# Decode attention with a streamed K and V cache: 64 KB rows in overlapping places instead of 32 KB rows in a ring of four

## The chip, the cores and the metric

The kernel runs on one core of one Trainium2 chip. The metric is the device time of one execution in microseconds. Before the change the median of three runs is 2530.58 us (2530.54 to 2530.72).

## What is computed

One token passes through two branches that a gate mixes: attention over a cache of 65536 keys and values for each of 32 heads, and a small gated MLP. The cut reference:

```python
def _A_ref(x, k_cache, v_cache, wq, wo):      # H = 32, Dh = 128, Sk = 65536, D = 512
    q = (x @ wq).reshape(B, Sq, H, Dh).transpose(0, 2, 1, 3)
    scores = jnp.einsum("bhqd,bhkd->bhqk", q, k_cache) * (Dh ** -0.5)
    p = _softmax(scores, axis=-1)
    o = jnp.einsum("bhqk,bhkd->bhqd", p, v_cache)
    return o.transpose(0, 2, 1, 3).reshape(B, Sq, H * Dh) @ wo

def _B_ref(x, w_gate, w_up, w_down):          # F = 1792
    return (_silu(x @ w_gate) * (x @ w_up)) @ w_down

g = _sigmoid((x * gate_w).sum(-1, keepdims=True))
return g * a + (1 - g) * b
```

All tensors are bf16. K and V hold 512 MiB each; every byte of them is read once, for one query row.

## The kernel before

**The stream.** K and V of a head are cut into four tiles (`t` = 0 to 3) of 4 MB. In a tile each of the 128 partitions holds `ROWS` = 128 successive keys of 128 numbers, one contiguous row of 32 KB in HBM. `ring` has `NPL` = 4 places of 32 KB in each partition. `plan_stream` (L26) writes the order of all loads by hand: wq, the first K tile, the MLP's weights, the other K tiles of head 0, then for each head h from 1 on its K tiles alternating with the V tiles of head h - 1, and at the end the four V tiles of the last head. Load n goes to place n mod 4. The loop L63 to L86 notes for each place the tile that it held before; the last three V tiles are cut in parts by `ENDS`, so that little is left to do after the last one lands.

**The issuing queue.** All loads are issued by SP, in order (`issue`, L190). Ahead of each it waits until the tile that held the place is worked off: a K tile by `ktdone` (its two transposes are done), a V tile by `pvdone` (its matmuls are done), a weight by the semaphore of its last use. Two tiles of K and two of V are in the ring at a time. The sixteen DMA engines work on one queue; an engine carries eight of a DMA's 128 rows and then a packet of 4 bytes that raises the semaphore.

**K.** DVE (`head_k`, L365) waits for a K tile and transposes it in two units of `UROWS` = 64 rows into `kt`, which has two buffers; a unit waits until PE has finished with the unit two before it (`qkdone`). PE (`scores`, L435) takes 16 matmuls for each unit, all 128 of a head accumulating in `psS`.

**Softmax.** After a head's last unit DVE takes the maximum over `psS` (`head_max`), GpSimd the maximum over partitions, ACT the exponential (`head_exp`), GpSimd the sum. `head_turn` transposes the probabilities on DVE after the first unit of the next head's K; `head_norm` takes the reciprocal of the sum after the fourth.

**V.** PE (`values`, L456) takes 32 matmuls of four rows each for a V tile, accumulating a head in `psO`. ACT scales the result (`row_norm`), PE turns it into a column (`turn`, L478), ACT stores the column. PE's loop (L519) runs `scores(1, t)` and `values(0, t)` in turn, so head h's V is worked off between the tiles of head h + 1's K.

**Start and end.** At the start PE computes q from wq; the MLP sits between units of head 0 (`mlp_up` after the first, `mlp_down` after the second). At the end the output weights wo are loaded into `kt` after the first V tile of the last head (L205), and `regroup`, `project_groups` and `project` multiply the heads' columns by them. The last V tile's matmuls go directly to the column `psT` (L473).

Of the kernel before, what the change touches and what calls it, by code (L numbers as in the profile page):

```python
# [5 lines left out]
P = 128  # L6
ROWS = 128
UROWS = 64
PLACE = ROWS * 128
UNIT = UROWS * 128  # L10
NPL = 4
NSEM = 8
STEP = 16
ENDS = {1: (64, 128), 2: (64, 128), 3: (64, 96, 112, 128)}
# [9 lines left out]


def plan_stream(H, PL):  # L26
    first = [("wq",), ("k", 0, 0), ("wg", "wu"), ("wd",)]
    first += [("k", 0, t) for t in range(1, PL)]
    steady = [(kind, h - d, t) for h in range(1, H) for t in range(PL) for kind, d in (("k", 0), ("v", 1))]
    last = [("v", H - 1, t) for t in range(PL)]  # L30
    return first, steady, last


def bass_gated_mix__mha_block_cached__swiglu_ffn__decode_kernel(
# [18 lines left out]
    PL = S // P // ROWS  # L53
    UN = 2 * PL
# [3 lines left out]
    assert Dh == 128 and D == 512 and F % P == 0 and PL == 4  # L58

    first, steady, last = plan_stream(H, PL)  # L60
    items = first + steady + last

    dmas = []  # L63
    landed = {}
    place = {}
    owner = [None] * NPL
    for n, item in enumerate(items):
        s = n % NPL
        if item[0] in "kv":
            place[item] = s  # L70
            parts = [(0, ROWS)]
            if item[:2] == ("v", H - 1) and item[2] in ENDS:
                parts = list(zip((0,) + ENDS[item[2]], ENDS[item[2]]))
            for r0, r1 in parts:
                landed[item + (r1,)] = len(dmas)
                dmas.append((item, r0, r1, s, owner[s]))
        else:
            for j, name in enumerate(item):
                place[name] = (s, j)
                landed[name] = len(dmas)  # L80
                dmas.append(((name,), 0, 0, s, owner[s]))
        owner[s] = item
        if item == ("v", H - 1, 0):
            for name in ("woa", "wob"):
                landed[name] = len(dmas)
                dmas.append(((name,), 0, 0, None, None))  # L86

    with ExitStack() as ctx:
# [6 lines left out]
        def sem(name):  # L95
# [9 lines left out]
        ring = sb("ring", [P, NPL, PLACE], BF16)  # L105
# [28 lines left out]

        tail = landed[("v", H - 1, 0, ROWS)]
        ds = [sem(f"ds{i}") for i in range(NSEM + len(dmas) - tail)]
        (s_x, s_ones, s_sel0, s_sel, s_unit0, s_unit, s_z, s_e1, s_xT, s_xTb, s_q, s_qTb, s_qs, s_qd, s_qz,
         s_qw, s_h, s_sig, s_gu, s_b, s_dch, ktdone, qkdone, pvdone, s_mx, s_ar, s_nb, expdone, s_pb, s_L,
         s_li, s_or, s_zr, s_zb, s_z4, s_sel4, s_x1, s_x2, s_pt, s_oc, s_otn, s_y, s_fin, s_out) = [sem(n) for n in (
             "s_x s_ones s_sel0 s_sel s_unit0 s_unit s_z s_e1 s_xT s_xTb s_q s_qTb s_qs s_qd s_qz "  # L140
             "s_qw s_h s_sig s_gu s_b s_dch ktdone qkdone pvdone s_mx s_ar s_nb expdone s_pb s_L "
# [16 lines left out]
        def weight(name):  # L158
            s, j = place[name]
            n = w_dram[name].shape[1]  # L160
            return ring[:, s, j * n:(j + 1) * n]

        wq_ap = weight("wq").rearrange("p (c n) -> p c n", c=Dc)
        wg_ap = weight("wg").rearrange("p (c m j) -> p c m j", c=Dc, j=FC)
        wu_ap = weight("wu").rearrange("p (c m j) -> p c m j", c=Dc, j=FC)
        wd_ap = weight("wd").rearrange("p (c n) -> p c n", c=FC)
        ktf = kt[:].rearrange("p b t -> p (b t)").bitcast(BF16)
        woa = ktf[:, 0:HN * D].rearrange("p (b m) -> p b m", b=HB)
        wob = ktf[:, HN * D:].rearrange("p (h n) -> p h n", n=D)
        ktb = [kt[:, b, :].bitcast(BF16).rearrange("p (j k m e) -> p j k m e", j=2, k=4, e=2) for b in range(2)]  # L170
# [3 lines left out]
        def counts(n):  # L174
            return (ds[n % NSEM], 16 * (n // NSEM + 1)) if n < tail else (ds[NSEM + n - tail], 16)

        def arrived(eng, n, more=0):
            sem_n, count = counts(n)
            eng.wait_ge(sem_n, count + more)  # L179

        def pv(h, t):
            return STEP * (h + 1) + 4 * (t + 1)
# [3 lines left out]
        @block.sync  # L186
        def _(sp):
            k_dram, v_dram = [c.rearrange("a h (b p r) d -> (a h b) p (r d)", p=P, r=ROWS) for c in (A_k_cache, A_v_cache)]

            def issue(n, q0=0):  # L190
                item, r0, r1, s, old = dmas[n]
                name = item[0]
                if old is not None and r0 == 0:
                    if old[0] == "k":
                        sp.wait_ge(ktdone, STEP * old[1] + 4 * (old[2] + 1) + 4 * q0)
                    elif old[0] == "v":
                        sp.wait_ge(pvdone, pv(old[1], old[2]) + 4 * q0)
                    else:
                        sp.wait_ge({"wq": s_q, "wg": s_h, "wd": s_b}[old[0]], 1)
                if name in ("k", "v"):  # L200
                    cache = k_dram if name == "k" else v_dram
                    src = cache[bass.ds(PL * item[1] + item[2] + q0, 1), :, r0 * Dh:r1 * Dh].rearrange("q p m -> (q p) m")
                    dst = ring[:, s, r0 * Dh:r1 * Dh]
                elif name in ("woa", "wob"):
                    sp.wait_ge(qkdone, STEP * H)  # L205
                    dst, src = (woa if name == "woa" else wob), wo_dram[name]
                else:
                    dst, src = weight(name), w_dram[name]
                sp.dma_start(dst, src).then_inc(counts(n)[0], 16)  # L209
                if n == 0:  # L210
                    sp.dma_start(xrow[0:1, :], xr_dram).then_inc(s_x, 16)  # L211
                    sp.dma_start(gwrow[0:1, :], gw_dram).then_inc(s_x, 16)  # L212

            turn_round = landed[("k", 2, 0, ROWS)]
            for n in range(turn_round):
                issue(n)
            with sp.Fori(0, PL * (H - 3) + 1, PL) as q0:
                for n in range(turn_round, turn_round + 2 * PL):
                    issue(n, q0)
            for n in range(tail, len(dmas)):  # L220
                issue(n)
# [29 lines left out]
        def _(act):  # L251
# [10 lines left out]
            def row_norm(h, more=0):  # L262
                act.wait_ge(s_li, STEP * (h + 1) + more)
                act.wait_ge(pvdone, pv(h, PL - 1) + more)
                act.wait_ge(s_pt, STEP * (h + 1) + more)
                nc.scalar.mul(orow[0:4, :], psO[0:4, :], Li[0:4, :]).then_inc(s_or, STEP)  # L266
# [32 lines left out]
            act.wait_ge(pvdone, pv(H - 1, PL - 2))  # L299
# [8 lines left out]
        def _(dve):  # L308
# [46 lines left out]
            def head_turn(h, more=0):  # L355
                dve.wait_ge(expdone, STEP * (h + 1) + more)
                dve.wait_ge(pvdone, pv(h - 1, PL - 1) + more)
                nc.vector.transpose(pb[:], pa[:]).then_inc(s_pb, STEP)  # L358
# [6 lines left out]
            def head_k(h, more=0):  # L365
                for u in range(UN):
                    i = h * UN + u
                    if u % 2 == 0:
                        arrived(dve, landed[("k", h, u // 2, ROWS)], more)
                    if i >= 2:  # L370
                        dve.wait_ge(qkdone, 2 * (i - 1) + more)  # L371
                    o = kt[:, i % 2, :].rearrange("p (j r t) -> p r j t", j=2, t=32)
                    src = ring[:, place[("k", h, u // 2)], (u % 2) * UNIT:(u % 2 + 1) * UNIT]
                    src = src.bitcast(U32).rearrange("p (r j t) -> p r j t", j=2, t=32)
                    nc.vector.transpose(o, src).then_inc(ktdone, 2)  # L375
                    if i == 1:
                        mlp_steps()
                    if u == 0 and h >= 1:
                        head_turn(h - 1, more)
                    if u == 3 and h >= 1:  # L380
                        head_norm(h - 1, more)
# [8 lines left out]
            dve.wait_ge(pvdone, pv(H - 1, PL - 1))  # L390
# [4 lines left out]
        def _(pe):  # L395
# [7 lines left out]
            arrived(pe, landed["wq"])  # L403
# [13 lines left out]
            def mlp_up():  # L417
                arrived(pe, landed["wg"])
                arrived(pe, landed["wu"])
# [7 lines left out]
            def mlp_down():  # L427
                arrived(pe, landed["wd"])
# [4 lines left out]
                done.then_inc(s_b, 1)  # L433

            def scores(h, t, more=0):  # L435
                for u in (2 * t, 2 * t + 1):
                    i = h * UN + u
                    pe.wait_ge(ktdone, 2 * (i + 1) + more)
                    if u == 0:
# [3 lines left out]
                    for k in range(4):  # L443
                        at0 = 31 - (4 * u + k)
                        for je in range(4):
                            done = nc.tensor.matmul(psS[:], qw[:, je, at0:at0 + 128],  # L446
                                                    ktb[i % 2][:, je // 2, k, :, je % 2],
                                                    start=(u == 0 and k == 0 and je == 0),
                                                    stop=(u == UN - 1 and k == 3 and je == 3))
                    done.then_inc(qkdone, 2)  # L450
                    if h == 0 and u == 0:
                        mlp_up()
                    if h == 0 and u == 1:
                        mlp_down()

            def values(h, t, more=0):  # L456
# [60 lines left out]
            for t in range(PL):  # L517
                scores(0, t)
# [47 lines left out]
```

## Time and profile before

| what | value |
|---|---|
| median of three runs | 2530.58 us |
| the profiled execution's own time | 2531.01 us |
| its span, first to last instruction | 2529.2 us |
| read from HBM | 1087.64 MB |
| PE busy, mean granted clock | 2028.8 us (80%), 0.927 |
| DVE busy | 1170.8 us (46%) |
| ACT busy, GpSimd busy | 69.0 us, 27.4 us |
| transposes of K (L375) | 256, 4424 ns each |
| matmuls of scores (L446) | 1080.7 us busy |
| matmuls of values (L468) | 898.6 us busy |
| maximum, exponential, probabilities' transpose | 32 each, 691, 687 and 671 ns |

Durations of single matmuls overlap, so the busy time of a group of them divided by their number says more than a matmul's own duration. The share of the DMA engines is a mean over all sixteen. The profiled execution's time stands beside its own span; the median is that of other executions.

### The profile page before, as it was taken

To read this page: it belongs to the slowest core of one execution; us is meant where nothing else is said; L and a number is where in the kernel's file an instruction comes from. 1 tells how busy PE (TensorE), PEld (TensorE's weight loads), DVE (VectorE), ACT (ScalarE), POOL (GpSimd) and SP (SyncE) were. 2 spreads that over 40 slices of the span, in tenths; PEclk is the share of its full clock that TensorE was granted. 3 is DMA by queue.
4 is the path that set the end of the run, shared out by engine and by line. 5 is a ranking of instruction groups with operands and counts; after the bars stand their busy time and mean duration, and the time that the engine had idled before them with its cause. 6 is when DMAs were issued, how large, how long until landed. Compare 5 with 4: busy or idle time off the path is not lost.

```text
span 2529.2 us, 20878 instructions
## 1 busy us (share of the span) xinstructions
PE 2028.8 (80%) x8736; PEld 813.5 (32%) x8864; DVE 1170.8 (46%) x374; ACT 69.0 (3%) x198; POOL 27.4 (1%) x80
## 2 busy tenths in 40 slices
PE   5888788787877877888778878787887788877888
PEld 3333233333333333333323333333333333333333
DVE  4644544454445444544454445444544454455441
ACT  0000000000000000000000000000000000000000
POOL 0000000000000000000000000000000000000000
PEclk9999989989999999899998998999999989999999
DMA  9999999999999999999999999999999999999999
GB/s 416 431 431 432 432 432 431 432 432 432 432 431 431 433 432 431 431 431 432 432 432 432 432 433 431 431 431 431 434 431 431 431 432 431 433 433 432 432 431 381
DMA packets 39614, 1087.78 MB, mean 430 GB/s; under 512 B 4275, under 2 KB 4790, under 8 KB 5942
## 3 DMA queue, kind: packets, MB, share of 16 engines
q1 hardware_dynamic: 39604, 1087.65, 100.0%
q8 instruction: 7, 0.11, 0.0%
q14 instruction: 1, 0.01, 0.0%
q10 hardware_dynamic: 2, 0.00, 0.0%
HBM read 1087.64 MB, written 0.00 MB: 430 GB/s over the span
## 4 chain that ended last, share of the span: by engine, by line
DMA 76%; DVE 12%; issue 11%; SPq 1%; PE 0%; DVEq 0%; ACT 0%
DMA ring<-in_A_k_cache_dram 75%; DVE kt L375 12%; DMA ring<-in_A_v_cache_dram 1%; SPq L209 1%; PE psS L446 0%; DVEq L371 0%; DVEq L362 0%; PE psY L491 0%; PE psT L473 0%; ACT fin L302 0%; SPq L211 0%; DVE oTn L391 0%; SPq L212 0%; DVEq L390 0%; DVEq L179 0%
## 5 line engine op out<-in xcount | busy, mean ns | idle before, releaser
L375 DVE STREAM_TRANSPOSE kt<-ring 128x4096 uint32<-128x4096 uint32 x256 | 1125.1, 4424 | 1142.5 <-DMA ring<-in_A_k_cache_dram 1138.7
L446 PE MATMUL psS<-kt,qw 128*128 128x512 bf16 x3968 | 1080.7, 431 | 478.2 <-DVE kt L375 472.9
L468 PE MATMUL psO<-ring,pb 128*4 128x512 bf16 x4064 | 898.6, 379 | 2.7 <-DMA ring<-in_A_v_cache_dram 2.7
L446 PEld LDWEIGHTS psS<-kt,qw 128*128 128x128 bf16 x4096 | 419.3, 106 | 1137.8 <-DVE kt L375 387.5
L468 PEld LDWEIGHTS psO<-ring,pb 128*4 128x4 bf16 x4064 | 343.4, 87 | 536.3 <-issue 41.2
L353 DVE TENSOR_REDUCE mxs<-psS 128x1 f32<-128x512 f32 x32 | 22.1, 691 | 142.6 <-PE psS L446 142.6
L260 ACT COPY qw<-qd 128x16 bf16 (+1 forms) x33 | 8.6, 260 | 2210.0 <-PE psS L446 2203.2
L246 POOL PARTITION_ALL_REDUCE amx<-mxs x32 | 11.3, 352 | 2397.4 <-DVE mxs L353 2397.4
L482 PEld LDWEIGHTS psT<-unit,orow 4*128 4x128 f32 x264 | 31.8, 186 | 15.2 <-issue 13.7
L482 PE MATMUL psT<-unit,orow 4*128 4x1 f32 x264 | 34.6, 248 | 0.9 <-ACT orow L300 0.5
L266 ACT ACTIVATE orow<-psO,Li 4x512 f32<-4x512 f32 x31 | 21.0, 679 | 138.4 <-PE psO L468 138.4
L358 DVE STREAM_TRANSPOSE pb<-pa 128x512 bf16<-128x512 bf16 x32 | 21.5, 671 | 6.3 <-PE psO L468 6.3
L280 ACT ACTIVATE pa<-psS,nbias 128x512 bf16<-128x512 f32 x32 | 22.0, 687 | 5.2 <-ACT nbias L276 5.1
L391 DVE TENSOR_SCALAR oTn<-psT,Li,zb 128x1 bf16<-128x1 f32 x1 | 0.3, 279 | 38.3 <-PE psT L473 38.3
L248 POOL PARTITION_ALL_REDUCE Lt<-rsum x32 | 12.3, 384 | 44.9 <-ACT pa L280 44.9
L400 PE MATMUL psM<-ones,xrow 1*128 1x1 bf16 x4 | 0.3, 172 | 13.3 <-DMA gwrow<-in_gate_w_dram 13.3
L270 ACT ACTIVATE oTn<-psT,zb 128x1 f32 (+1 forms) x32 | 8.2, 255 | 1.1 <-PE psT L482 1.1
L276 ACT ACTIVATE nbias<-amx 128x1 f32<-128x1 f32 x32 | 6.5, 203 | 33.3 <-POOL amx L246 33.3
L423 PEld LDWEIGHTS psM<-xTb,ring 128*128 128x128 bf16 x112 | 6.9, 161 | 0.2
L423 PE MATMUL psM<-xTb,ring 128*128 128x1 bf16 x112 | 6.8, 198 | 0.0
L510 PE MATMUL psY<-kt,oX 128*1 128x512 bf16 x28 | 6.2, 379 | 0.0
L280 ACT ACTIVATION_READ_ACCUMULATOR pa<-psS,nbias 128x1 f32 x32 | 6.2, 193 | 0.0
(51 smaller groups left out, 42.5 us busy)
## 6 DMA issues: line engine op xcount, KB each, us to landing
ring<-in_A_k_cache_dram SPq DMA_DIRECT2D x128, 4096.0 KB, 29.7
ring<-in_A_v_cache_dram SPq DMA_DIRECT2D x125, 4096.0 KB, 27.7
ring<-in_A_v_cache_dram SPq DMA_DIRECT2D x5, 2048.0 KB, 23.5
ring<-in_A_wq_dram SPq DMA_DIRECT2D x1, 4096.0 KB, 12.3
kt<-in_A_wo_dram SPq DMA_DIRECT2D x1, 3584.0 KB, 14.7
ring<-in_B_w_gate_dram SPq DMA_DIRECT2D x1, 1792.0 KB, 26.0
ring<-in_B_w_up_dram SPq DMA_DIRECT2D x1, 1792.0 KB, 29.8
ring<-in_B_w_down_dram SPq DMA_DIRECT2D x1, 1792.0 KB, 33.6
```

The costliest lines, as they stand in the source:

```text
L209: sp.dma_start(dst, src).then_inc(counts(n)[0], 16)
L246: nc.gpsimd.partition_all_reduce(amx[:], mxs[:], P, RMAX).then_inc(s_ar, STEP)
L248: nc.gpsimd.partition_all_reduce(Lt[:], rsum[:], P, RADD).then_inc(s_L, STEP)
L266: nc.scalar.mul(orow[0:4, :], psO[0:4, :], Li[0:4, :]).then_inc(s_or, STEP)
L280: nc.scalar.activation(pa[:], psS[:], ACT.Exp, bias=nbias[:], scale=SCALE, accum_out=rsum[:]).then_inc(expdone, STEP)
L353: nc.vector.reduce_max(mxs[:], psS[:], AX_X).then_inc(s_mx, STEP)
L358: nc.vector.transpose(pb[:], pa[:]).then_inc(s_pb, STEP)
L375: nc.vector.transpose(o, src).then_inc(ktdone, 2)
L423: done = nc.tensor.matmul(psM[:, o + j:o + j + 1], w[:, c, :, j], xTb[:, c:c + 1], start=(c == 0), stop=(c == Dc - 1))
L446: done = nc.tensor.matmul(psS[:], qw[:, je, at0:at0 + 128], ktb[i % 2][:, je // 2, k, :, je % 2], start=(u == 0 and k == 0 and je == 0), s ...
L468: done = nc.tensor.matmul(psO[0:4, :], pbk[:, k, rho:rho + 4], v[:, r * Dh:(r + 4) * Dh], start=(t == 0 and r == 0), stop=(t == (PL - 1 if ...
L482: done = nc.tensor.matmul(psT[:, 0:1], orow[0:4, i * Dh:(i + 1) * Dh], unit[0:4, i:i + 1], start=(i == 0), stop=(i == 3 and h < H - 1))
```

## The change

K and V no longer share a ring. K has `kr`, 96 KB in each partition, V has `vr`, 80 KB. A head's K and V come in two tiles (`b` = 0, 1) of 8 MB, a row of 64 KB (256 keys) in each partition. The two places of K lie at 0 and at 32 KB of `kr` and share 32 KB; the two places of V lie at 0 and at 16 KB of `vr` and share 48 KB. So a tile can be loaded when the shared part of the tile before it is worked off, and the tiles are worked off with this part first: `K_ORDER` for K, in eight units of 32 rows (`UP` = 8), and `V_ORDER` for V, in quarters of 64 rows. `kt` shrinks by half with the unit, and `ktdone`, `qkdone` and `pvdone` count finer steps; `pv(h, n)` stands for n of head h's eight quarters of V. SP's order is written out: in the loop K b=0, V b=0, K b=1, V b=1, one wait ahead of each.

Head 0's K comes in four halves of 4 MB, the first two ahead of the MLP's weights, which go to `vr`, and the third one behind a wait for four units. The MLP's matmuls all come after the twelfth unit of head 0. The output weights go to `kr`, ahead of the last head's V, which comes in parts (`LAST`); its first tile goes to K's second place. `turn` now follows a head's first unit, and the end runs regroup, the projections and then the last head's values.

The diff, cut to its core:

```diff
+HALF = 128
+ROWS = 2 * HALF
+UROWS = 32
+QROWS = 64
+K_AT = (0, PLACE // 2)
+V_AT = (0, PLACE // 4)
+V_ORDER = ((1, 2, 3, 0), (0, 1, 2, 3))
+LAST = {0: (128, 192, 256), 1: (64, 128, 192, 224, 240, 256)}
...
+    K_ORDER = (tuple(range(UP // 2, UP)) + tuple(range(UP // 2)), tuple(range(UP)))
...
-        ring = sb("ring", [P, NPL, PLACE], BF16)
+        kr = sb("kr", [P, 3 * PLACE // 2], BF16)
+        vr = sb("vr", [P, 5 * PLACE // 4], BF16)
...
-            turn_round = landed[("k", 2, 0, ROWS)]
-            for n in range(turn_round):
-                issue(n)
-            with sp.Fori(0, PL * (H - 3) + 1, PL) as q0:
-                for n in range(turn_round, turn_round + 2 * PL):
-                    issue(n, q0)
-            for n in range(tail, len(dmas)):
-                issue(n)
+            load(("wq",), w_at["wq"], w_dram["wq"])
+            sp.dma_start(xrow[0:1, :], xr_dram).then_inc(s_x, 16)
+            sp.dma_start(gwrow[0:1, :], gw_dram).then_inc(s_x, 16)
+            first_k(0, HALF, ROWS)
+            first_k(0, 0, HALF)
+            load(("wg",), w_at["wg"], w_dram["wg"])
+            sp.wait_ge(ktdone, UP // 2)
+            first_k(1, 0, HALF)
+            load(("wu",), w_at["wu"], w_dram["wu"])
+            load(("wd",), w_at["wd"], w_dram["wd"])
+            first_k(1, HALF, ROWS)
+            with sp.Fori(0, 2 * (H - 2) + 1, 2) as q0:
+                more = q0 * (STEP // 2)
+                for b in range(2):
+                    sp.wait_ge(ktdone, STEP + (-UP // 2, UP // 2)[b] + more)
+                    load(("k", b), k_rows(b, 0, ROWS), cache_rows(k_dram, 1, b, 0, ROWS, q0))
+                    sp.wait_ge(pvdone, (pv(-1, 7), pv(0, 3))[b] + more)
+                    load(("v", b), v_rows(0, b, 0, ROWS), cache_rows(v_dram, 0, b, 0, ROWS, q0))
+            sp.wait_ge(ktdone, STEP * (H - 1) + UP)
+            load(("woa",), woa, wo_dram["woa"])
+            load(("wob",), wob, wo_dram["wob"])
+            sp.wait_ge(ktdone, STEP * H)
+            for b in range(2):
+                if b == 1:
+                    sp.wait_ge(pvdone, pv(H - 2, 8))
+                for r0, r1 in zip((0,) + LAST[b], LAST[b]):
+                    load(("vl", b, r1), v_rows(H - 1, b, r0, r1), cache_rows(v_dram, H - 1, b, r0, r1))
...
             def head_k(h, more=0):
-                for u in range(UN):
-                    i = h * UN + u
-                    if u % 2 == 0:
-                        arrived(dve, landed[("k", h, u // 2, ROWS)], more)
+                for n in range(UN):
+                    i = h * UN + n
+                    b, w = n // UP, K_ORDER[n // UP][n % UP]
+                    if h == 0 and n % (UP // 2) == 0:
+                        dve.wait_ge(landing(("k0", b, w * UROWS)), 16)
+                    if h > 0 and n % UP == 0:
+                        dve.wait_ge(landing(("k", b)), 16 * h + more)
                     if i >= 2:
-                        dve.wait_ge(qkdone, 2 * (i - 1) + more)
+                        dve.wait_ge(qkdone, i - 1 + more)
...
-                for r in range(0, ROWS, 4):
...
+                order = V_ORDER[b] if h < H - 1 else (0, 1, 2, 3)
+                if h < H - 1:
+                    pe.wait_ge(landing(("v", b)), 16 * (h + 1) + more)
+                for n, c in enumerate(order):
+                    for r in range(c * QROWS, (c + 1) * QROWS, 4):
...
+                    done.then_inc(pvdone, 2)
...
             with pe.Fori(0, STEP * (H - 1), STEP) as more:
-                for t in range(PL):
-                    scores(1, t, more)
-                    if t == 0:
-                        turn(-1, more)
-                    values(0, t, more)
+                for b in range(2):
+                    scores(1, b, more)
+                    values(0, b, more)
```

## The prediction

> **What bounds the kernel now.** I read the page's slices first, then the queue's share, the chain of waits, and last the waits of the issuing queue. In the slices and the queue table one resource has no free tenth:
>
> ```profile
> span 2529.2 us, 20878 instructions
> PE   5888788787877877888778878787887788877888
> DVE  4644544454445444544454445444544454455441
> DMA  9999999999999999999999999999999999999999
> DMA packets 39614, 1087.78 MB, mean 430 GB/s; under 512 B 4275, under 2 KB 4790, under 8 KB 5942
> q1 hardware_dynamic: 39604, 1087.65, 100.0%
> DMA 76%; DVE 12%; issue 11%; SPq 1%; PE 0%; DVEq 0%; ACT 0%
> ```
>
> PE and DVE have holes in every slice; the sixteen DMA engines have none. The chain lies on K landings. Its DVE and issue shares are no cost of their own: during them the issuing queue SP is ahead of the engines. The waits of SP from 400 to 2400 us, and the issue table, show by how much:
>
> ```profile
> SPq L209 <- PE psO L468: 1153.5, 103, 13.0
> SPq L209 <- DVE kt L375: 730.7, 103, 8.6
> ring<-in_A_k_cache_dram SPq DMA_DIRECT2D x128, 4096.0 KB, 29.7
> ring<-in_A_v_cache_dram SPq DMA_DIRECT2D x125, 4096.0 KB, 27.7
> ```
>
> A 4 MB DMA lands 28 to 30 us after its issue, and the stream gives one about every 9.7 us, so about two others are ahead of each: the queue never runs dry. So only two things can move the time: the time an engine needs per byte, and a hole in the queue. The stream's pace is read where DVE starts a head, on a K landing:
>
> ```profile
> 1008.88 4.45 DVE L375 STREAM_TRANSPOSE kt<-ring 128x4096 uint32<-128x4096 uint32 x1 [5.51 <-DMA ring<-in_A_k_cache_dram]
> 1086.60 4.45 DVE L375 STREAM_TRANSPOSE kt<-ring 128x4096 uint32<-128x4096 uint32 x1 [5.14 <-DMA ring<-in_A_k_cache_dram]
> 1164.34 4.45 DVE L375 STREAM_TRANSPOSE kt<-ring 128x4096 uint32<-128x4096 uint32 x1 [5.14 <-DMA ring<-in_A_k_cache_dram]
> 1242.06 4.45 DVE L375 STREAM_TRANSPOSE kt<-ring 128x4096 uint32<-128x4096 uint32 x1 [6.02 <-DMA ring<-in_A_k_cache_dram]
> ```
>
> (1242.06 - 1008.88) / 3 = 77.73 us a head, eight DMAs of 4 MB, 9.716 us each: 431.7 GB/s. On one engine such a DMA is eight packets of 32 KB and one of 4 bytes that raises the semaphore.
>
> **What a packet costs beyond its bytes.** I read the trace's packet records, start to start on one engine: 1214 ns for 32 KB and 611 ns for 16 KB (the last V places); 308.6 ns for 8 KB and 156.4 ns for 4 KB. The 4-byte packet pushes the next one back by 6 ns: 8 x 1214 + 6 = 9718, the 9.716 us above. Two packets of 16 KB take 2 x 611 - 1214 = 8 ns more than one of 32 KB. Averaged over all records of the two sizes the difference is 6.8 ns, and two 8 KB against one of 16 KB give 6.7. The records' own durations (1217.5 and 615 ns) would give 12.5, but they overlap the next start by 3 to 4 ns. So a packet costs 7 to 12.5 ns whatever its size; I take 8, since the starts are what the stream goes by.
>
> The Trainium skill, "DMA: Bandwidth & Descriptors", section "Why small descriptors are slow (HBM only)", has a fixed cost of about 3 cycles a packet besides 32 bytes of descriptor. At that page's 850 MHz and 27.2 bytes per ns I estimate 4.7 ns, which would make the gain 5.4 us where mine is 8.7; the starts in this trace are dearer than the page.
>
> **The change, part by part.**
>
> *Rows of 64 KB in the loop.* 31 rounds of four DMAs are 124 DMAs of 8 MB, in place of 248 of 4 MB. The trace of before has no 64 KB packet. Bounds for what each engine saves per 8 MB: below, nothing but the second semaphore packet, 6 ns; above, 8 x 12.5 + 6 = 106 ns. Taken: 8 x 8 + 6 = 70 ns, since 64 KB continues the row of sizes. Times 124: 8.7 us, with ends 0.7 and 13.1. Head 0, the weights and the last V keep 32 KB rows or smaller, in the same sizes and number as before.
>
> *Places free by parts.* One DMA is in flight and one is queued, where about two were. An 8 MB DMA takes 19.36 us. The costs at nothing hold only while SP gets each next DMA out early, so I work out both waits from a K landing at 0. From issue to first packet take 1.3 us (SP's first issue at 0.73, its packets from 1.76 on), and from the last packet to the landing seen by an engine up to 1.5 us (packets behind the first K start at 21.6 to 22.6, DVE at 24.07).
>
> K's second place waits for four units of 32 rows on DVE: half of the 4424 ns of the transpose group each, 8.8 us. It must be issued by 19.4 - 1.5 - 1.3 = 16.6: 7.8 us to spare. The V place loaded after it waits for three quarters of the V before: PE starts these when the eight units of scores are done, at 8 x 2.2 + 1.9 (eight matmuls, 3.78 us for sixteen) + 1.05 for turn = 20.6, then 48 matmuls at 221 ns (898.6 us / 4064): 31.2. It must be issued by 38.7 - 2.8 = 35.9: 4.7 to spare. The wait on V's second place has the same sum without turn. Queued behind either wait on SP is only the next DMA, whose own wait ends later anyway. So zero, covered by the transfer in flight. At the head's end, reduce, all-reduce and exp take under 4 us (1080.77 to 1083.2) and their transpose of the probabilities comes after the first unit of the next K, 38 us on: covered.
>
> *DVE and PE in half units.* 512 transposes in place of 256. Even at 0.1 us fixed each that is 26 us on an engine busy for 1171 of 2529: nothing, hidden under the stream. PE's matmuls are the same in number.
>
> *The start.* K's second place of head 0 now waits for four units while only wq, two K halves and wg are queued. wg's packets now begin at 21.6 to 22.6, behind one K; one more 4 MB (9.7) and wg (8 x 541 ns = 4.3) let the queue run out at 35.6 to 36.6. DVE begins at 24.07, but PE's first matmuls take 427 ns each (29.15, 29.58, 30.00), 3.4 us a unit, and DVE may be only two units ahead: units end at 26.3, 28.5, 32.1, 34.4 to 35.5. With 1.3 us the first packet comes at 35.7 to 36.8: a hole of 0 to 1.2 us. Taken: 0.3. mlp_down then frees the V ring at about 72, 12 us ahead of need.
>
> *The end.* The output weights are issued a K place earlier and into K's ring, behind a K half long transposed, and the last V parts have the sizes they had; from the last landing to the end nothing changes. Zero, bounds -1 to 1.
>
> **Sum.** The profiled execution took 2531.0, its span of 2529.2 and 1.8 around it: 2531.0 - 8.7 + 0.3 = 2522.6. It lay 0.4 above the median of the runs, 2530.58, so the forecast is **2522.2**. Its own range goes from 13.1 saved to 7.5 saved with the largest hole and 1 us at the end: 2517 to 2525.3.
>
> **Rivals.**
>
> *No gain.* If rows of 64 KB are cut into two packets, or a packet's cost grows with its length, only the semaphore packets are gone: 2530.6 - 0.7 + 0.3 = 2530.2. For it: no size above 32 KB is on record. Against: the same 7 to 8 ns at each doubling from 8 KB on.
>
> *V's place comes free too late.* One mechanism, at SP's wait ahead of a V load. PE's clock was granted 0.927 of full speed on average; the clock records know only 1 and 0.5, in stretches of 3.4 or 6.8 us, so 15% of the time at half. After the change PE works from 2.3 to 34.8 and idles about 6 us in a place pair of 38.7, where the gaps on K were 3.6 to 4.8, so half speed may come at every K landing. A stretch of 3.4 us puts PE back 1.7 us; the spare 4.7 are gone after 9.4 us at half speed per pair, against 5.8 now. Each us beyond that in delay is a hole, 62 times: three stretches, 10.2 us, make 0.4 x 62 = 25 us, 2547; four, 2.1 x 62 = 130. Against: two stretches cost nothing, and a PE that ends late has a shorter gap after it.
>
> The Trainium skill, "TensorE: Matmul & The Clock Gate", "Part 1: The HAM clock gate", halves the clock after an idle window of about 3.4 us and restores it after a busy one; by it alone each K place would open with one or two slow windows, still inside the spare.
>
> *Longer pitch reads slower.* Neighbouring partitions' rows now lie 64 KB apart in HBM, not 32. The nearest row is wo, 4 KB packets from pieces 512 KB apart: 160.5 ns start to start, against 156.4 for 4 KB of V, 2.6% more. At 1% the stream loses 25 us: 2547 less 8.7, 2539; at 2.6%, 2579. Against: packets of V at pitch 32 KB and of the weights at 14 KB keep one pace per byte.
>
> The Trainium skill, "DMA: Bandwidth & Descriptors", "Latency and other measured facts", reports a loss at row pitches of large powers of two, 207 against 214 GB/s at 512 KiB and far more from 2 MiB; nothing there is as short as 64 KB.
>
> **How the numbers follow.** Forecast 0.71; no gain 0.14; V late 0.09; pitch 0.06. 0.2% is 5.1 us, about what a measurement of this kernel can tell from no change: the forecast's whole own range lies below 2525.5, no gain inside, the last two above 2535.6. So faster 0.71, same 0.14, slower 0.15. The range goes from 2516.5, the upper bound of the gain, past no gain to 2533; it leaves out the two slow cases.
>
> **What would show it.** Queue q1 should have 39604 - 124 x 144 = 21748 packets; about 37600 would say that rows are cut. The head's period should fall from 77.73 to 77.73 - 4 x 0.07 = 77.45 us, and the slices show about 433 GB/s. SP should still wait before each DMA of the loop, and a K landing should come some 28 us after its issue; 21 us would say that the queue ran dry. It is wrong if the period falls with fewer than 0.1 us, if the DMA row has an 8, or if the start loses over 2 us.

## The result and the profile after

The changed kernel takes 2541.62 us (median of 7 executions, 2538.19 to 2552.96), the kernel before 2530.72 (2530.54 to 2531.23): a ratio of 1.0049, 95% interval 1.0033 to 1.0065. It is slower by 11 us, and where the kernel before repeats to 0.7 us the changed one scatters over 15. The profiled execution took 2541.62, its span is 2539.8.

The page of the changed kernel, the lines that answer to those of before (the tenths of the granted TensorE clock and the GB/s in 40 slices of the span, then the queue table and the shares of the chain):

```profile
span 2539.8 us, 21029 instructions
PEclk9888989989988999899898899998888989889889
DMA  9999999999999999999999999999999999999999
GB/s 413 429 431 431 429 423 424 437 433 431 429 428 429 429 429 425 428 436 429 436 433 428 420 436 428 437 432 426 429 432 427 430 430 430 439 429 430 418 430 380
DMA packets 21758, 1087.77 MB, mean 428 GB/s; under 512 B 2291, under 2 KB 2806, under 8 KB 3958
q1 hardware_dynamic: 21748, 1087.65, 99.6%
DMA 69%; PE 16%; DVE 12%; issue 3%; SPq 0%; DVEq 0%; ACT 0%
```

The queue has exactly the 21748 packets that rows of 64 KB make. But its share is 99.6%, not 100.0%, the slices wander between 418 and 439 where before they stood at 431 to 434, and PE has entered the chain of waits with 16%: some of what releases the stream is now PE's work.

The waits of SP from 400 to 2400 us (total, number, longest) come to 1940 us, where they were 1884, so SP is idle as much as before; the question is when each wait ends:

```profile
SPq L166 <- PE psO L456: 1059.6, 51, 22.3
SPq L166 <- DVE kt L357: 880.6, 52, 22.1
```

Here is one K place that opens a head, from the timeline (start, duration, engine, line, what, in brackets the idle time before it and what ended it):

```profile
1024.70 2.31 DVE L357 STREAM_TRANSPOSE kt<-kr 128x2048 uint32<-128x2048 uint32 x1 [17.23 <-DMA kr<-in_A_k_cache_dram]
1027.24 3.59 PE L429 MATMUL psS<-kt,qw 128*128 128x512 bf16 x8 [6.66 <-DVE kt L357]
1030.76 1.86 PE L470 MATMUL psT<-unit,orow 4*128 4x1 f32 x8
1036.19 2.31 DVE L357 STREAM_TRANSPOSE kt<-kr 128x2048 uint32<-128x2048 uint32 x1 [3.01 <-PE psS L429]
1038.67 0.33 SPq L166 DMA_DIRECT2D kr<-in_A_k_cache_dram  x1
1049.30 13.98 PE L456 MATMUL psO<-vr,pb 128*4 128x512 bf16 x64
1060.01 0.33 SPq L166 DMA_DIRECT2D vr<-in_A_v_cache_dram  x1
1063.61 4.50 DVE L357 STREAM_TRANSPOSE kt<-kr 128x2048 uint32<-128x2048 uint32 x2 [16.28 <-DMA kr<-in_A_k_cache_dram]
```

PE comes out of 6.66 us of idleness and takes 3.59 us for eight matmuls that later take 1.98; then come the eight small matmuls of turn (L470), 1.86 us where 1.05 was reckoned; DVE waits 3.01 us for PE. The scores end at 1049.3, 24.6 us after the landing instead of 20.6, and the V load goes out at 1060.01, 35.3 us after it instead of 31.2. The next K is seen landed at 1063.61.

What follows is in the windows (length, busy time and number of PE, PEld, DVE, ACT and GpSimd, granted clock, share of the DMA engines, GB/s), one question asked about the clock and one about the stream:

```profile
1024.70:1036.10 11.40, 8.63 (x24) 4.06 (x26) 7.41 (x4) 0.00 (x0) 0.00 (x0) 0.55 1.05 454
1036.10:1049.30 13.20, 11.67 (x48) 4.04 (x46) 11.14 (x6) 0.00 (x0) 0.00 (x0) 1.00 1.00 432
...
1000.00:1060.00 60.00, 50.88 (x208) 20.02 (x211) 23.88 (x14) 2.07 (x6) 0.73 (x2) 0.91 1.00 435
1060.00:1065.00 5.00, 3.28 (x16) 1.13 (x13) 1.39 (x1) 0.00 (x0) 0.00 (x0) 1.00 1.04 406
1065.00:1140.00 75.00, 62.48 (x260) 23.88 (x264) 35.76 (x19) 2.07 (x6) 0.73 (x2) 0.93 1.00 433
```

For its first 11.4 us the place has 0.55 of the clock: the clock records show half speed from 1025.9 to 1036.1, three stretches of 3.41 us in a row. And around 1060 to 1065 the stream falls to 406 GB/s beside 435 and 433. A window of 5 us counts whole packets where they start, and windows without a hole read 419 to 446 by that, so this reading is rough; the spacing of the landings is the better one.

Over the run, K landings without a hole come 38.70 us apart, against 4 x 9.716 = 38.86 us for the same bytes before: 0.16 us better for each 16 MB, or 82 ns for each 8 MB DMA, 10.2 us in all. From head 1 on, 60 distances exceed 38.70 by 19.8 us together; below this sum is called the excess. The span is 2539.8 - 2529.2 = 10.6 us longer: 19.8 of holes less 10.2 of cheaper packets, and 1.0 us that is left for the start, the last landing and the end. A head takes 77.40 us where no hole falls and 78.06 on average, where it took 77.73 before.

The holes lie where V is issued late. I set each V issue's delay behind the K landing beside the holes, and the time at half clock in the 31 us behind the landing:

| K place | V issued behind the landing, mean (latest) | time at half clock, mean |
|---|---|---|
| first of a head | 34.5 us (36.1) | 9.3 us |
| second of a head | 31.8 us (32.7) | 3.9 us |

22 V loads went out more than 34.5 us behind the landing, at 34.9 to 36.1, all at first places: exactly the 22 of 31 with 10.2 us or more at half clock. The other nine have 6.6 or less and issue by 33.1.

### The profile page after: what moved, and what is told of

Same layout as the page of the kernel before. It is cut to its first block, busy times and chain, and to the rows that moved or that the text cites. A ratio compares the mean times of both kernels' runs of the same rounds, so it can differ in the third digit from the quotient of the medians.

```text
span 2539.8 us, 21029 instructions
## 1 busy us (share of the span) xinstructions
PE 2079.5 (82%) x8737; PEld 809.9 (32%) x8864; DVE 1192.9 (47%) x630; ACT 68.9 (3%) x198; POOL 27.1 (1%) x80
## 3 DMA queue, kind: packets, MB, share of 16 engines
q1 hardware_dynamic: 21748, 1087.65, 99.6%
## 4 chain that ended last, share of the span: by engine, by line
DMA 69%; PE 16%; DVE 12%; issue 3%; SPq 0%; DVEq 0%; ACT 0%
DMA kr<-in_A_k_cache_dram 68%; PE psS L429 13%; DVE kt L357 12%; PE psT L470 2%; DMA vr<-in_A_v_cache_dram 1%; PE psO L456 1%; SPq L166 0%; DVEq L353 0%; PE psT L461 0%; PE psY L479 0%; ACT fin L281 0%; SPq L175 0%; DVE oTn L373 0%; SPq L176 0%; DVEq L372 0%
## 5 line engine op out<-in xcount | busy, mean ns | idle before, releaser
L357 DVE STREAM_TRANSPOSE kt<-kr 128x2048 uint32<-128x2048 uint32 x512 | 1148.4, 2286 | 1202.6 <-DMA kr<-in_A_k_cache_dram 1057.2
L429 PE MATMUL psS<-kt,qw 128*128 128x512 bf16 x3969 | 1119.4, 428 | 438.5 <-DVE kt L357 428.7
L456 PE MATMUL psO<-vr,pb 128*4 128x512 bf16 x4000 | 873.8, 379 | 1.9 <-DMA vr<-in_A_v_cache_dram 1.9
L429 PEld LDWEIGHTS psS<-kt,qw 128*128 128x128 bf16 x4096 | 391.8, 104 | 1138.9 <-issue 408.3
L456 PEld LDWEIGHTS psO<-vr,pb 128*4 128x4 bf16 x4000 | 343.0, 87 | 528.8 <-issue 24.3
L470 PEld LDWEIGHTS psT<-unit,orow 4*128 4x128 f32 x264 | 50.3, 280 | 25.9 <-issue 24.7
L470 PE MATMUL psT<-unit,orow 4*128 4x1 f32 x264 | 53.1, 318 | 0.8 <-ACT orow L245 0.4
L456 PE MATMUL psO<-kr,pb 128*4 128x512 bf16 x64 | 14.0, 379 | 0.0
L382 PE MATMUL psM<-ones,xrow 1*128 1x1 bf16 x4 | 0.3, 172 | 13.6 <-DMA gwrow<-in_gate_w_dram 13.6
L255 ACT ACTIVATE nbias<-amx 128x1 f32<-128x1 f32 x32 | 6.5, 203 | 33.3 <-POOL amx L225 33.3
L405 PEld LDWEIGHTS psM<-xTb,vr 128*128 128x128 bf16 x112 | 6.9, 158 | 0.2
L405 PE MATMUL psM<-xTb,vr 128*128 128x1 bf16 x112 | 6.8, 198 | 0.0
## 6 DMA issues: line engine op xcount, KB each, us to landing
vr<-in_A_wq_dram SPq DMA_DIRECT2D x1, 4096.0 KB, 12.5
kr<-in_A_wo_dram SPq DMA_DIRECT2D x1, 3584.0 KB, 31.6
vr<-in_B_w_gate_dram SPq DMA_DIRECT2D x1, 1792.0 KB, 34.9
```

The source lines that it names most:

```text
L357: nc.vector.transpose(o, src).then_inc(ktdone, 1)
L405: done = nc.tensor.matmul(psM[:, o + j:o + j + 1], w[:, c, :, j], xTb[:, c:c + 1], start=(c == 0), stop=(c == Dc - 1))
L429: done = nc.tensor.matmul(psS[:], qw[:, je, at0:at0 + 128], ktb[i % 2][:, je // 2, k, :, je % 2], start=(n == 0 and k == 0 and je == 0), s ...
L456: done = nc.tensor.matmul(psO[0:4, :], pbk[:, k, rho:rho + 4], v_rows(h, b, r, r + 4), start=(b == 0 and n == 0 and r == c * QROWS), stop= ...
L470: done = nc.tensor.matmul(psT[:, 0:1], orow[0:4, i * Dh:(i + 1) * Dh], unit[0:4, i:i + 1], start=(i == 0), stop=(i == 3 and h < H - 1))
```

## The experiments

**Theory A**: PE's clock halves in the idle time ahead of a K landing; at a head's first place the small matmuls of turn keep it down for a third stretch, V's place comes free too late, and the queue has holes. **Theory B**: the holes come from the shallow queue of two large DMAs, whatever PE does. **Theory C**: rows 64 KB apart in HBM read slower.

All medians are beside the kernel before on the same chip, 2530.99, 2530.95 and 2530.97 us in the three sets of runs (2530.48 to 2531.51 over all).

### turn moved

```diff
                     done.then_inc(qkdone, 1)
-                    if h >= 1 and n == 0:
-                        turn(h - 2, more)
...
                 for b in range(2):
                     scores(1, b, more)
                     values(0, b, more)
+                    if b == 0:
+                        turn(-1, more)
```

> The changed kernel with turn moved from behind the first unit of a head to behind the values of its first V tile. Theory A (PE at half clock makes the V load late: three slow windows at a head's first K place, because turn's small matmuls keep the window from counting as busy, put SP's V issue 35 us behind the K landing, and about 20 us of holes follow): half clock at that place falls from 10.2 to 3.4 us, the V issue comes under 33 us behind the landing, the holes go: 2520 to 2524 us. Theory B (the holes come from having only one 8 MB DMA queued, whatever PE does): no change, 2538 to 2545. Theory C (rows 64 KB apart read slower): no change, 2538 to 2545.

Measured: 2523.78 us (2521.98 to 2524.82), ratio 0.9972 (0.9962 to 0.9983). Moving eight small matmuls takes 18 us off the changed kernel. The place that answers to the one above, from the timeline of this kernel:

```profile
1015.27 2.31 DVE L357 STREAM_TRANSPOSE kt<-kr 128x2048 uint32<-128x2048 uint32 x1 [15.85 <-DMA kr<-in_A_k_cache_dram]
1017.80 7.97 PE L429 MATMUL psS<-kt,qw 128*128 128x512 bf16 x24 [5.28 <-DVE kt L357]
1036.84 13.98 PE L454 MATMUL psO<-vr,pb 128*4 128x512 bf16 x64
1047.54 0.33 SPq L166 DMA_DIRECT2D vr<-in_A_v_cache_dram  x1
1050.75 1.05 PE L468 MATMUL psT<-unit,orow 4*128 4x1 f32 x8
```

The V load goes out 32.3 us behind the landing, and turn takes its 1.05 us where nobody waits. Half clock at first places is 6.2 us on average, not the 3.4 that I expected: two stretches instead of three. The latest V issue is 33.0, and the excess over 38.70 is 0.3 us in all. The slices of this execution and its queue:

```profile
GB/s 412 436 432 433 434 435 434 433 433 436 435 433 434 434 433 433 434 433 433 434 433 434 435 433 433 434 435 433 434 433 433 436 433 435 434 433 434 433 433 379
q1 hardware_dynamic: 21748, 1087.65, 99.9%
```

432 to 436 between the first slice and the last: rows 64 KB apart read faster than those 32 KB apart did, which ends theory C, and the queue has the same depth as in the changed kernel, which ends theory B.

### PE kept busy

```diff
                     values(0, b, more)
+                    for _ in range(20):
+                        nc.tensor.matmul(psW[:], sel[:, 0, :], sel[:].rearrange("p e m -> p (e m)"),
+                                         start=True, stop=True)
```

`psW` is a PSUM bank that nothing reads; the diffs from here on leave out its declaration.

> The changed kernel with 20 idle matmuls (4.4 us, into a PSUM bank that nothing reads) behind the values of each V tile in the loop, so that PE is never idle for a whole 3.4 us window; turn stays where it is. Theory A: clock 0.98 or more, V issue 32 us behind the landing at both places, no holes, 2519 to 2523 us, and the spread between executions (15 us) falls under 1 us, since it came from where the windows lie. Theory B and theory C: no change, 2538 to 2545, with the same spread.

Measured: 2527.96 us (2525.77 to 2534.2), 0.9989 (0.998 to 0.9998): turn stays and most of the holes go, so the clock is the cause. But the figures miss on the high side. The excess is 2.9 us, not nothing: the clock is 0.975, half speed still comes for 2.5 us at first places, and one V goes out at 35.3; executions scatter by 8 us, not by less than one. And the end is longer: the stream's last packet ends at 2520.9, the span at 2527.5, 6.6 us later where before it was 4.3. The idle matmuls behind the last V tile in the loop stand ahead of the end's work on PE:

```profile
2486.01 4.49 PE L512 MATMUL psW<-sel 128*128 128x512 bf16 x20
2490.34 0.56 PE L490 MATMUL psQ<-oTn,sel 128*128 128x7 bf16 x16
```

### Both

The two edits together, with 22 idle matmuls.

> turn moved as in the first run, and 22 idle matmuls behind each V tile's values, so both causes of lateness are gone. Theory A: V issues 30 to 32 us behind the K landing, no holes, 2520 to 2524 us; whatever is left above 2520 lies at the start or the end. If holes come from anything but PE's lateness, it stays where the first run was or above, 2524 to 2530.

Measured: 2525.53 us (2524.66 to 2526.54), 0.9978 (0.9969 to 0.9987), above the expected range and inside the one set for holes from another source. In the loop it is as expected: V issues at 31.6 and 30.3 us behind the landing, excess 0.1 us. The rest is the end, 7.0 us from the last packet where the run before has 6.6, and a hole of 2.0 us near 36 us, where SP waits for head 0's first four units.

### Wide matmuls in turn's place

```diff
                     done.then_inc(qkdone, 1)
                     if h >= 1 and n == 0:
-                        turn(h - 2, more)
+                        for _ in range(5):
+                            nc.tensor.matmul(psW[:], sel[:, 0, :], sel[:].rearrange("p e m -> p (e m)"),
+                                             start=True, stop=True)
```

turn itself stands behind the first V tile as in the first run.

> turn moved as in the first run, and in the place it had, behind the first unit of every head, and behind the first unit of the second K tile too, five idle matmuls of 512 columns, which take turn's time (1.1 us at full clock, 2.1 at half) but keep PE busy. If turn hurts by holding the clock down (theory A as put): half clock stays at 6.8 us or less, V issues at 33 to 34.5 us, 2523 to 2528 us. If it hurts by its time alone: V issues at 35 as in the changed kernel, 2538 to 2545.

The expectation is wrong in one detail: the five matmuls stand only behind a head's first unit. Measured: 2523.77 us (2522.44 to 2525.73), 0.9971 (0.9961 to 0.9982). V issues at first places come at 33.3 us (latest 34.1), 1.0 later than without them, with 6.5 us at half clock. The profiled execution, the slowest of the eight, has 1.7 us of excess; the median is that of the first run. So about the same time on PE costs nothing in the median when it is spent on wide matmuls, and 18 us when it is spent on turn: turn does harm by holding the clock down, as theory A says.

### V later, with nothing else changed

```diff
                 for b in range(2):
                     scores(1, b, more)
+                    if b == 0:
+                        for _ in range(10):
+                            nc.tensor.matmul(psW[:], sel[:, 0, :], sel[:].rearrange("p e m -> p (e m)"),
+                                             start=True, stop=True)
                     values(0, b, more)
```

with turn moved as in the first run.

> turn moved as in the first run, and ten idle matmuls (2.2 us) between a head's first eight units of scores and the values of the V tile behind them: the V issue is put back by 2.2 us at each head's second place, with no change to the clock or to turn. Theory A: issues come 34 to 35.2 us behind the K landing, half of the heads get holes again of 0.3 to 1 us: 2528 to 2542. Theory B (lateness is not the cause): 2522 to 2525 as in the first run.

The expectation names second places; the edit stands behind the scores of a head's first tile, and the run puts V back at first places. Measured: 2534.06 us (2529.14 to 2538.43), 1.0011 (1.0002 to 1.002). V issues at first places come at 34.5 us on average, the latest at 35.1, 16 beyond 34.5, and the excess is 9.7 us. Lateness alone, with 6.7 us at half clock where the first run had 6.2, brings the holes back, and the scatter with them (9 us). Over six profiles, the changed kernel's and those of the five experiments so far (58 places in each; the first and the last three are left out), the distance of K landings into which the late V's transfer falls exceeds 38.70 by:

| V issued behind the K landing | places | mean excess | largest |
|---|---|---|---|
| 30.0 to 33.5 us | 280 | 0.01 us | 0.41 us |
| 33.5 to 34.5 us | 32 | 0.12 us | 0.78 us |
| 34.5 to 35.0 us | 14 | 0.36 us | 1.16 us |
| 35.0 us and later | 22 | 0.84 us | 1.99 us |

### What the rows are worth

Two runs cut the loop's loads into two DMAs of 32 KB rows, under the same waits: in the changed kernel, and with turn moved. The diff is cut to the loads; DVE and PE then wait for both halves.

```diff
-                    load(("k", b), k_rows(b, 0, ROWS), cache_rows(k_dram, 1, b, 0, ROWS, q0))
+                    for r in (0, HALF):
+                        load(("k", b, r), k_rows(b, r, r + HALF), cache_rows(k_dram, 1, b, r, r + HALF, q0))
...
-                    load(("v", b), v_rows(0, b, 0, ROWS), cache_rows(v_dram, 0, b, 0, ROWS, q0))
+                    for r in (0, HALF):
+                        load(("v", b, r), v_rows(0, b, r, r + HALF), cache_rows(v_dram, 0, b, r, r + HALF, q0))
```

> The changed kernel with each 8 MB load of the loop issued as two DMAs of 4 MB, rows of 32 KB, under the same wait; places, units and waits as they are. Theory A: the 82 ns saved per 8 MB are given back (124 x 82 ns = 10 us), the holes stay or shrink a little as each place takes 0.16 us longer: 2546 to 2552 us. Theory B: two shorter DMAs queued close most holes: 2530 to 2535. Theory C (only the distance of rows matters): 2541 plus the second semaphore packets, 2540 to 2545.

Measured: 2547.42 us (2539.4 to 2551.28), 1.0056 (1.0042 to 1.007). The holes stay and the packets cost more again; two shorter DMAs don't close them, against theory B.

> turn moved as in the first run and the loop's loads cut into two DMAs of 32 KB rows: the overlapping places alone, with a queue without holes. Theory A: the first run's time and the packets' price, 124 x 82 ns = 10.2 us: 2532 to 2535 us, some us above the kernel before. If a part of the gain comes from the places or from fewer waits and not from the rows: under 2530.

Measured: 2533.03 us (2531.62 to 2533.81), 1.0007 (0.9998 to 1.0017). Beside the first run this is 9.25 us for 124 x 2 DMAs in place of 124: 75 ns for 8 MB, 6 of them the semaphore packet, so 8.6 ns a packet. The overlapping places alone gain nothing; all that the change can gain is in the rows.

The third is the kernel before with halves of its rows (the diff is cut; the readers wait for both semaphores):

```diff
+                if n < tail:
+                    m = dst.shape[1] // 2
+                    sp.dma_start(dst[:, :m], src[:, :m]).then_inc(counts(n)[0], 16)
+                    sp.dma_start(dst[:, m:], src[:, m:]).then_inc(ds2[n % NSEM], 16)
+                else:
+                    sp.dma_start(dst, src).then_inc(counts(n)[0], 16)
```

> The kernel before with every tile and weight ahead of the last V issued as two DMAs of half rows: 16 KB in place of 32 KB for K and V. It measures what a packet costs by itself in a queue that never runs dry. Theory A, by the starts of the packets: (8 x 8 + 6) ns x 248 = 17 us more, 2546 to 2549. If the cost grows with the bytes, only the semaphore packets: 2532 to 2533. By the records' durations: (8 x 12.5 + 6) ns x 248 = 26 us, 2556 to 2558.

Measured: 2549.58 us (2549.51 to 2550.11), 1.0074 (1.006 to 1.0088), just above the range. The edit cuts every load ahead of the last head's V, 256 DMAs and not the 248 of the expectation (the queue has 76468 - 39604 = 256 x 144 packets more). 18.6 us more for 256 is 73 ns each, 8.3 ns a packet. The slices of this kernel stand at 428 and 429:

```profile
GB/s 410 428 428 429 429 428 428 428 428 429 429 428 429 429 429 428 428 429 429 429 429 429 429 428 428 429 428 429 429 429 429 428 428 428 428 429 429 428 429 386
```

### A version that beats both

```diff
+            load(("wu",), w_at["wu"], w_dram["wu"])
             sp.wait_ge(ktdone, UP // 2)
             first_k(1, 0, HALF)
-            load(("wu",), w_at["wu"], w_dram["wu"])
```

This is to close the hole at the start. With turn moved, and once with 22 idle matmuls ahead of each K tile's scores, once without them:

> turn moved as in the first run, 22 idle matmuls ahead of each K tile's scores in the loop (so none at the kernel's end), and the load of wu issued ahead of SP's first wait on K, so that 4.3 us more are queued there. Theory A: no holes in the loop, none near 36 us, end as in the kernel before: the kernel before less 124 x 82 ns, 2519.5 to 2522 us, spread under 1.5 us. If the lateness of PE had a further source: 2523 or more.

Measured: 2522.32 us (2521.89 to 2524.06), 0.9968 (0.9956 to 0.998), a little above the range, and the executions scatter by 2.2 us, not by less than 1.5.

> the run before without the idle matmuls: turn moved and wu ahead of the first wait. Theory A: the hole near 36 us, 0.4 to 2 us in the runs so far, goes, and the loop has next to no holes, as in the first run: 2520.5 to 2523 us, 1 to 2 under the first run. If that hole cost nothing: 2523 to 2525.

Measured: 2522.61 us (2521.8 to 2523.16), 0.9967 (0.9955 to 0.9979). The idle matmuls add nothing that can be told once turn has moved. The hole near 36 us is gone in both; another, 0.6 and 0.8 us, stands at 64 us, ahead of the loop's first load. In the first run's profile the one near 36 us was about 0.65, and its executions, 2521.98 to 2524.82, overlap with these, so a gain of this edit over turn moved alone isn't shown. The first of the two in its clock and its queue:

```profile
PEclk9999999999999999999999999999999999999999
GB/s 416 434 433 433 433 433 433 434 434 433 434 433 434 435 436 433 435 434 434 433 433 435 434 433 433 433 433 434 433 434 434 433 433 435 434 434 435 434 433 377
```

Both are 8.4 to 8.7 us faster than the kernel before: what the forecast had for the changed kernel, 8.4, is reached by one in which V comes in time.

## Why the prediction was wrong

**What bounds the kernel**, and the rule that only the time per byte and holes in the queue can move it: right. The result is the sum of just these two.

**The price of a packet**: right in kind, a little small. I took 8 ns and 70 ns for each 8 MB, 8.7 us; two runs give 8.3 and 8.6 ns, 73 and 75 ns, and the spacing of landings in the changed kernel gives 82 ns, 10.2 us. The packets' starts were the right row to go by; their durations (12.5 ns) were too dear. The Trainium skill, "DMA: Bandwidth & Descriptors", section "Why small descriptors are slow (HBM only)", with about 3 cycles a packet and 32 bytes of descriptor, is too low here: the 4.7 ns that I estimated from it stand against 8.3 to 8.6 measured.

**Places free by parts, at nothing**: this is the step that failed, on both sides of its comparison. The reckoned V issue, 31.2 us behind the landing, holds for a PE at full clock: with PE kept busy and turn moved, second places issue at 30.3 us, where I had 30.2, and first places, with some half clock left, at 31.6. But I let the half clock stand as a rival with the spare of 4.7 us to absorb it. In the run, 22 of the 31 first places had three stretches or more at half speed and issued V at 34.9 to 36.1 us. I gave the idle time of PE the right size, 6 us (6.66 in the timeline), and didn't ask what the matmuls behind it would do for the clock. And the limit was too late: I counted back from the last packet of the K ahead, and allowed 35.9. In the table above the losses are small up to 34.5 and grow beyond it. The account that fits is that the first engine to finish must have the next packet, and the engines finish 2 to 2.5 us apart (below). With turn moved, where hardly a hole disturbs the queue, the first of a K's sixteen semaphore packets starts 3.1 us ahead of the landing (2.9 to 3.2), and a late V's first packet follows its issue by about 1.0 us: 38.7 - 3.1 - 1.0 = 34.6. The trace of before has both rows already: there too the first semaphore packet starts 3.1 us ahead of a K landing on average, and from SP's first issue at 0.73 to its packets at 1.76 are 1.0 us, not the 1.3 that I took. My 1.5 us from the last packet to the landing missed the last engine, whose semaphore packet starts at 23.52, 0.55 ahead of the 24.07.

**The rival "V's place comes free too late"**: the right mechanism, at the right wait, with 0.09 for a chance. Its price for three stretches was 25 us, 0.4 at each of 62 places; the run has 19.8 us, some 0.9 at each of 22, so that the two totals lie near each other is luck. With the measured term in the sum, 2530.6 - 8.7 + 0.3 + 19.8 = 2542.0, beside 2541.6 measured; the term is read off this trace, so that bears out the account and not the forecast.

**"Longer pitch" and "no gain"**: both wrong. Rows 64 KB apart read at 432 to 436 GB/s once the holes are gone.

**The start**: a hole of 0.3 us taken, 0 to 1.2 the bounds; it was 0.4 us in the changed kernel and up to 2.0 in experiments with the same start. **The end**: nothing taken, 4.3 us from the last packet to the end as before. **DVE in half units**: 512 of 2286 ns against 256 of 4424, 1148 against 1125 us busy, 23 us more where I allowed 26, and hidden.

## What to carry to other kernels

A stream at its ceiling has only two things to win, the price of its packets and its holes; when a change buys the first with depth of queue, reckon the release of each place at half the PE clock, and don't count on narrow matmuls like turn's, which here didn't bring the clock back. Count the spare to the moment at which the first DMA engine runs out, not to the landing. And where a kernel's executions scatter by 15 us and used to repeat within one, look for a wait that has lost its cover and ends late only sometimes; here that was the cause.

## What the runs showed that was not expected

**Which work brings the clock back.** At first places, with turn's eight matmuls of 4 x 128 by one column behind the first unit, half speed lasts three stretches of 3.41 us or more at 22 of 31. With turn moved away, or with wide matmuls in its place, it comes to 6.2 and 6.5 us on average there, two stretches. At second places of the changed kernel, where no turn follows, it usually lasts one stretch; but PE is idle for 3.7 us on average ahead of these and for 6.8 us ahead of first places, so the two kinds of place differ in more than turn. With turn moved, second places have 4.5 us of idle time ahead, counted from turn's end, and two stretches, 5.9 us on average. The comparison at like idle time is with the run that puts V later. There the place that answers to the one above has 6.68 us of idle time ahead and half speed from 1019.2 to 1026.0, two stretches, and V goes out 34.5 us behind the landing:

```profile
1018.77 2.31 DVE L358 STREAM_TRANSPOSE kt<-kr 128x2048 uint32<-128x2048 uint32 x1 [17.25 <-DMA kr<-in_A_k_cache_dram]
1021.31 7.97 PE L430 MATMUL psS<-kt,qw 128*128 128x512 bf16 x23 [6.68 <-DVE kt L358]
1053.29 0.33 SPq L167 DMA_DIRECT2D vr<-in_A_v_cache_dram  x1
```

The Trainium skill, "TensorE: Matmul & The Clock Gate", section "Part 1: The HAM clock gate", has the clock halved after an idle window of about 3.4 us and restored after a busy one; the stretches in this trace agree in length (3.41, 6.83 and 10.24 us). By that rule a window with turn in it did not count as busy; no record shows what a window counts.

**The engines of one DMA don't finish together.** For the K that lands at 1063.61 in the changed kernel, the sixteen 4-byte packets in the trace's records start between 1061.24 and 1063.15, and the landing is seen 0.46 us behind the last. The V issued at 1060.01 has its first packet at 1061.24, 1.2 us later; nine engines were through by 1061.5. The engine that sets the landing goes from K to V at 1063.15 without a pause, and nevertheless time was lost: this landing comes 38.91 us behind the one ahead. The loss is small here; the largest distances are 40.6 and 40.7 us.

**A hole costs more than its idle time.** In the windows above, 1060 to 1065 has a DMA share of 1.04 and 406 GB/s: the engines are busy and move less. The records show packets of 64 KB that start together around such a place taking 2.8 to 3.3 us, where 2.42 is usual. Over the run 248 of the 15872 records of 64 KB are longer than 2.8 us, and 4 with turn moved; the mean is 2435.5 ns against 2421.8, and for the 992 such packets of an engine that is 13.6 us. The stream, from its first packet to its last, is 19.7 us longer than with turn moved, so the larger part of what the holes cost lies in longer packets. Why they are longer was not tried.

**The scatter.** The clock's stretches begin on a grid of 3.41 us, and a head takes 77.4 us, 22.7 of these: where the landings fall on the grid differs from head to head. That this sets how often V comes late in one execution was not tested by itself. What the runs show is that the scatter goes with the late V and not with the clock: the five runs whose latest V issue in the loop is 33.0 us or less (turn moved, both, turn moved with two DMAs, and the last two) scatter by 1.4 to 2.8 us at clocks from 0.915 to 0.982. The run with PE kept busy has a clock of 0.975 and one V at 35.3 in its profile, and scatters by 8 us; the one with V put back scatters by 9.
